# A fused attention and expert kernel whose main loop is emitted in the order of planned times

## The chip, the cores and the metric

The kernel runs on one core of one Trainium2 chip. The metric is the device time of one execution in microseconds (us), the median of three runs. In what follows PE is TensorE (matmuls), PEld its weight loads, DVE is VectorE, ACT is ScalarE, POOL is GpSimd and SP is SyncE, which issues DMAs. Each engine works its own instructions strictly in the order in which the program emitted them; engines wait for each other by semaphores.

## What is computed

```python
qn = q / (norm(q, axis=1) + 1e-6);  kn = k / (norm(k, axis=1) + 1e-6)
a = softmax(kn.transpose(0, 2, 1) @ qn / tau)          # per batch, 256 x 256
x = (v @ a).reshape(12032, 256)                        # 2 batches of 6016 tokens
h = x @ w_in                                           # 256 -> 2048
g = maximum(h, 0) + alpha * minimum(h, 0)
out = g @ w_out                                        # 2048 -> 256
```

All tensors are fp32.

## The kernel before, in words

The kernel folds the 256 x 256 attention matrix of a batch into `w_in`, so that only two large products per token are left. Each fp32 operand is split into a high part (a rounding cast) and a low part (the difference), and every product is three matmul passes (`passes`, lines L115, L116, L117; the plain second product has them at L830).

**Tiles and items.** The 12032 tokens are 24 tiles of 500 or 504 tokens (12 a batch), and the 2048 hidden features are 8 pairs of 128-blocks. One tile with one pair is an *item*; there are 192, numbered i = 8 t + j for tile t and pair j. The first product of an item is a scheme of seven half-width products instead of eight. The second product is plain (twelve 500-column matmuls) in tiles 0 to 12 and 23, and in tiles 13 to 22 (`S_TILES`) it is seven products in the items with even j (*S items*) and plain in those with odd j.

**The steps of item i**, by function:

- PE `pe_a` (six 250-column matmuls into PSUM tile q), ACT `copies` (q to the accumulators r0, L605, and to p7, L606), PE `pe_b` (six into r0), DVE `add_p7(i, 0)` (r0 + p7 into r1, L622).
- one loop step later: PE `pe_c` (six, into r1 and r0; it needs `add_p7(i, 0)`), DVE `add_p7(i, 1)` (L622, needs pe_c), PE `pe_d` (three, into r0; it may start only when `add_p7(i, 1)` has read r0), then for each half `act_n` (ACT, L635) and `dve_g` (DVE, L644), which make g.
- two loop steps later: the split of g. Plain: `g_high` (ACT, gh, L653) and `g_low` (DVE, gl, L657). S items: `x_high`, `x_low` (xh, xl), `g_sums` (three DVE sums into t), `t_low` (ACT, and a DMA issued by POOL), `t_high` (ACT, L722, tgh).
- three and four loop steps later (`LAG = 3`): the second product, in two halves: `stage2`'s five and seven matmuls for a plain tile, `s2_first` and `s2_second` in the tiles 13 to 22, which sum into the PSUM banks X0 to X3.

**Tile ends.** A tile of S_TILES ends with `combine` (ACT copy of X2, L786; DVE L787, L788, L793, which give c) and `finish_out` for two halves (DVE L800, into ob, then the store); only then are the banks free for the next tile. These stand in the items j = 2 and j = 3 of the next tile. Beside them the v data of a later tile are prepared: `v_sums` (DVE), `v_high` (ACT L343, and two DMAs issued by POOL), `v_low` (DVE L349).

**What sets the order.** Nothing reorders the program (`manual_schedule`). The loop over items emits the calls in a fixed sequence written by hand; work beside the main line (weights, norms of batch 1, v) is put on lists `side`, `early` and `late` by item number. So each engine's queue is the projection of this text on that engine.

Of the kernel before, what the change touches and what calls it, by code (L numbers as in the profile page):

```python
# [25 lines left out]
def fused_kernel(
# [637 lines left out]
    ws, xs_t, ts_t, tt_t, started, cb_t = [], {}, {}, {}, set(), {}  # L664
# [23 lines left out]
    def g_sums(i):

        g = g_t[i]  # L690
        h = half_of(i)
# [151 lines left out]
    with tc.manual_schedule():  # L843
# [133 lines left out]

        at_item(NPAIR, a1.evac)
        i = NPAIR + 4
        for p in range(len(pieces)):  # L980
# [16 lines left out]
        at_item(i, lambda: (a1.sums_T(), a1.norms()))  # L997
        at_item(i + 2, bcast1)
        at_item(i + 3, lambda: a1.exps())
        at_item(i + 5, transposes1)  # L1000
        assert i + 5 <= last0 - 3, (i, last0)
        for j in range(NPAIR):

            i = last0 + 2 + 11 * j // 7
# [6 lines left out]
            at_item(i + 1, lambda j=j: m_split(a1, j))
        for n in range(len(S_J)):
            at_item(last0 + (14, 16, 19, 21)[n], s_weights, n)
        early, late = {}, {}
        for t in S_TILES:
            i = (t + 1) * NPAIR - 1 + LAG
            late[i] = [lambda t=t: combine(t)]
            early[i + 1] = [lambda t=t: finish_out(t, 0)]
# [18 lines left out]
        def pe_s2(s2):  # L1037
            if s2 is not None:
                next(s2, None)
            else:  # L1040
                pe_fill()

        for i in range(NI + LAG):

# [4 lines left out]
            if s_two:
                x_high(i - 2)  # L1050
                g_sums(i - 2)
            elif two:
                g_high(i - 2, 1)
                g_high(i - 2, 0)
                g_low(i - 2, 1)
            if new:
                pe_a(i)
                copies(i)
            if one:
                pe_c(i - 1)  # L1060
                add_p7(i - 1, 1)
            if s_two:
                x_low(i - 2)
            elif two:
                g_low(i - 2, 0)
            if in_s(i - LAG - 1):
                s2_second(i - LAG - 1)
            if s2 or i < LAG:
                pe_s2(s2)
            if one:  # L1070
                act_n(i - 1, 1)
                dve_g(i - 1, 1)
            for f in early.get(i, []):
                f()
            if s_two:
                t_low(i - 2)
            if one:
                pe_d(i - 1)
            if new:
                pe_b(i)  # L1080
                add_p7(i, 0)
            if one:
                act_n(i - 1, 0)
                dve_g(i - 1, 0)
            if s_two:
                t_high(i - 2)
            for f, args in side.get(i, []):
                f(*args)
# [41 lines left out]
```

## Time and profile before

| | us |
|---|---|
| median of 3 timed runs | 1160.81 (1156.49 to 1161.18) |
| the profiled execution's own time | 1163.18 |
| its span in the profile | 1161.4 |
| PE busy in it | 1122.4 |
| DVE busy | 921.3 |
| ACT busy | 843.5 |

The profile is of one execution. Of the table, the span is the stretch from the first to the last instruction; the execution's own time is 1.8 us longer. The busy time of PE is the union of its matmuls with ends that are modelled, since they overlap in the array.

### The profile page before, as it was taken

How to read it: one execution, taken by the hardware profiler on the slowest of the kernel's cores; microseconds unless marked ns; L12 is line 12 of the kernel's file. 1: busy time of each engine (PE TensorE's matmuls, PEld its weight loads, DVE VectorE, ACT ScalarE, POOL GpSimd, SP SyncE). 2: the span in 40 equal slices, each digit the busy share in tenths (PEclk: the TensorE clock that was granted, in tenths of full speed). 3: DMA queues.
4: the chain of work that ended last, by engine and by line, in shares of the span. 5: the costliest groups of instructions: out<-in, count | busy, mean ns of one | idle time of the engine just before them, and what ended most of it. 6: DMA issues, size and time to landing. Idle time of an engine off the chain costs nothing.

```text
span 1161.4 us, 19221 instructions
## 1 busy us (share of the span) xinstructions
PE 1122.4 (97%) x7284; PEld 1022.3 (88%) x7284; DVE 921.3 (79%) x1693; ACT 843.5 (73%) x1498; POOL 92.8 (8%) x118
## 2 busy tenths in 40 slices
PE   9999999999999999999999989999999999999988
PEld 8888888988988988899898878988988989889887
DVE  6798876777777777777798888888988888988865
ACT  6788677777777767667777677767767677777664
POOL 0000000000000000000002241011011011011000
PEclk9999999999999999999999999999999999999999
DMA  9996122232232011101101033343343343333310
GB/s 333 361 337 220 36 72 89 72 106 74 79 99 79 27 36 54 27 28 54 36 19 37 19 89 81 77 94 71 79 101 71 73 91 78 82 87 76 70 36 19
DMA packets 54589, 103.59 MB, mean 89 GB/s; under 512 B 5088, under 2 KB 30944, under 8 KB 54496
## 3 DMA queue, kind: packets, MB, share of 16 engines
q1 hardware_dynamic: 36224, 70.01, 17.8%
q0 software_dynamic: 18272, 32.34, 13.9%
q8 instruction: 58, 0.95, 0.4%
q14 instruction: 35, 0.29, 0.1%
HBM read 57.68 MB, written 12.32 MB: 60 GB/s over the span
## 4 chain that ended last, share of the span: by engine, by line
PE 79%; DVE 11%; ACT 7%; issue 2%; DMA 0%; SPq 0%; ACTq 0%; DVEq 0%
PE o L830 23%; PE r L115 8%; PE r L117 8%; PE r L116 8%; PE S L401 6%; PE X L115 5%; PE X L117 4%; PE X L116 4%; PE q L116 3%; PE q L115 3%; PE q L117 3%; ACT g L635 2%; DVE r L622 2%; DVE gl L657 2%; DVE g L644 1%
## 5 line engine op out<-in xcount | busy, mean ns | idle before, releaser
L635 ACT ACTIVATE g<-r,salpha 128x500 f32<-128x500 f32 (+1 forms) x384 | 260.6, 680 | 137.4 <-DVE r L622 82.1
L644 DVE SCALAR_TENSOR_TENSOR g<-r,sgn,g 128x500 f32<-128x500 f32 (+1 forms) x384 | 282.8, 736 | 36.8 <-ACT g L635 36.7
L830 PE MATMUL o<-gh,wo 128*128 128x500 f32 (+2 forms) x904 | 296.5, 389 | 3.0 <-DVE ob L800 3.0
L115 PE MATMUL r<-vs,m 128*128 128x250 f32 (+1 forms) x960 | 272.9, 284 | 22.8 <-DVE r L622 22.7
L117 PE MATMUL r<-vs,m 128*128 128x250 f32 (+1 forms) x960 | 268.6, 280 | 0.0
L116 PE MATMUL r<-vs,m 128*128 128x250 f32 (+1 forms) x960 | 268.5, 280 | 0.0
L622 DVE TENSOR_TENSOR r<-r,p 128x250 f32<-128x250 f32 (+1 forms) x384 | 163.2, 425 | 128.5 <-PE r L117 125.0
L657 DVE TENSOR_TENSOR gl<-g,gh 128x500 fp32r<-128x500 f32 (+1 forms) x304 | 206.1, 678 | 27.9 <-ACT gh L653 26.5
L115 PEld LDWEIGHTS r<-vs,m 128*128 128x128 f32 x960 | 182.0, 190 | 41.5 <-DVE r L622 34.7
L653 ACT CAST gh<-g 128x500 fp32r<-128x500 f32 (+1 forms) x304 | 177.0, 612 | 32.1 <-DVE g L644 31.0
L116 PEld LDWEIGHTS r<-vs,m 128*128 128x128 f32 x960 | 182.0, 190 | 4.7
L830 PEld LDWEIGHTS o<-gh,wo 128*128 128x128 f32 x904 | 162.0, 188 | 26.6 <-DVE ob L800 3.8
L117 PEld LDWEIGHTS r<-vs,m 128*128 128x128 f32 x960 | 181.9, 189 | 0.0
L830 PE MATMUL o<-gl,wo 128*128 128x500 f32 (+2 forms) x452 | 175.4, 388 | 0.0
L605 ACT COPY r<-q 128x500 f32<-128x500 f32 (+1 forms) x192 | 109.4, 570 | 60.4 <-PE q L117 60.3
L115 PE MATMUL q<-vs,m 128*128 128x250 f32 (+1 forms) x384 | 110.1, 287 | 0.0
L116 PE MATMUL q<-vs,m 128*128 128x250 f32 (+1 forms) x384 | 109.1, 284 | 0.6 <-DVE vs L349 0.6
L117 PE MATMUL q<-vs,m 128*128 128x250 f32 (+1 forms) x384 | 108.9, 284 | 0.3 <-DVE m L111 0.3
L830 PEld LDWEIGHTS o<-gl,wo 128*128 128x128 f32 x452 | 84.9, 188 | 13.6
L341 POOL DMA_DIRECT2D vs<-vt x46 | 33.6, 733 | 669.7 <-PE q L117 393.2
L116 PEld LDWEIGHTS q<-vs,m 128*128 128x128 f32 x384 | 74.7, 194 | 6.9 <-DVE vs L349 0.9
L115 PEld LDWEIGHTS q<-vs,m 128*128 128x128 f32 x384 | 74.3, 194 | 6.1
(144 smaller groups left out, 1772.3 us busy)
## 6 DMA issues: line engine op xcount, KB each, us to landing
tgl<-t POOLq DMA_DIRECT2D x28, 500.0 KB, 4.6
kqT<-kqT_dram SPq DMA_DIRECT2D x20, 512.0 KB, 3.6
kq<-k_dram SPq DMA_DIRECT2D x39, 256.0 KB, 5.6
kq<-q_dram SPq DMA_DIRECT2D x39, 256.0 KB, 5.7
v<-vT_dram SPq DMA_DIRECT2D x16, 500.0 KB, 4.3
vs<-vt POOLq DMA_DIRECT2D x32, 250.0 KB, 2.6
outT_dram<-ob SPq DMA_DIRECT2D x30, 250.0 KB, 2.0
tgl<-t POOLq DMA_DIRECT2D x12, 504.0 KB, 4.6
```

Source lines behind the costliest of these rows:

```text
L115: nc.tensor.matmul(out, wh, xh, start=first, stop=False, **s)
L116: nc.tensor.matmul(out, wh, xl, start=False, stop=False, **s)
L117: nc.tensor.matmul(out, wl, xh, start=False, stop=last, **s)
L341: nc.gpsimd.dma_start(out=v_spl[t][:, 0, sl, :h], in_=x)
L401: nc.tensor.matmul(self.S[cc], t[:, 0, j, cc * P : cc * P + P], t[:, 1, j, :], start=ci == 0 and j == 0 and not (self.shared and cc), stop ...
L605: nc.scalar.copy(r_t[i][0][:, :, :h], x[:, 0:1, :h].broadcast_to([P, 2, h]))
L622: nc.vector.tensor_tensor(out=r[1][:, n, :h], in0=r[0][:, 1, :h], in1=p7_t[i][:, :h], op=ALU.add)
L635: nc.scalar.activation(blocks(g_t[i], i, 2 * fi, 2 * fi + 2), r_t[i][fi][:, :, : half_of(i)], AF.Copy, scale=salpha[:, f : f + 1],)
L644: nc.vector.scalar_tensor_tensor(out=g, in0=r_t[i][fi][:, :, : half_of(i)], scalar=sgn[:, f : f + 1], in1=g, op0=ALU.mult, op1=ALU.max,)
L653: nc.scalar.copy(gs_t[i][0][:, fi, :w], g_t[i][:, fi * w : fi * w + w])
L657: nc.vector.tensor_tensor(out=gs_t[i][1][:, fi, :w], in0=g_t[i][:, fi * w : fi * w + w], in1=f32(gs_t[i][0][:, fi, :w]), op=ALU.subtract,)
L830: nc.tensor.matmul(o, x, y, start=first, stop=last or shared, skip_group_check=shared)
```

## The change

The loop no longer calls the steps; it puts each into a list `plan` with a planned time (item number times `PERIOD`, plus an offset), and at the end the list is sorted by that time and called. The offsets come from a table `ORDER` with one entry for each kind of loop step: *plain* (tiles 0 to 12 and 23), *sums* (the step in which the S item i - 2 is split) and *none* (the other steps of tiles 13 to 22). The numbers serve as sort keys only: no instruction is added, removed or moved to another engine. `g_sums` is cut into its three instructions, `combine` and `s_weights` into two calls each, so that the parts can be placed apart. In the loop steps of the plain kind, pe_c stands ahead of pe_a; before, pe_a was ahead of pe_c in every step.

```diff
+PERIOD = 5.0
+SIDE = 3.7
+ORDER = {
+    "plain": dict(
+        pe_c=0.0, add=(3.0, 0.1), high=(0.3, 0.2), pe_a=0.7, copy=0.8, low=(1.1, 1.0),
...
+TILE = dict(copy=3.42, sums=4.41, out0=1.24, out1=3.0)
...
-    def combine(t):
-
+    def combine_copy(t):
         h = tiles[t][2] // 2
         c = cb_t[t] = raw.tile([P, 2 * TW], F32, tag="raw", name=f"c{t}")
+        nc.scalar.copy(c[:, 3 * h : 4 * h], bank(t, 2)[:, :h])
+
+    def combine(t):
+
+        h = tiles[t][2] // 2
+        c = cb_t[t]
         p2, p3 = bank(t, 2), bank(t, 3)
         tt = nc.vector.tensor_tensor
-        nc.scalar.copy(c[:, 3 * h : 4 * h], p2[:, :h])
...
+        plan = []
+
+        def put(i, at, f, *args):
+            plan.append((i * PERIOD + at, len(plan), f, args))
+
+        def side(i, f, *args):
+            put(i, SIDE, f, *args)
...
         for n in range(len(S_J)):
-            at_item(last0 + (14, 16, 19, 21)[n], s_weights, n)
-        early, late = {}, {}
+            i = last0 + (14, 16, 18, 20)[n]
+            put(i, SIDE, s_weights, n)
+            put(i + 2, SIDE, s_weights_split, n)
         for t in S_TILES:
             i = (t + 1) * NPAIR - 1 + LAG
-            late[i] = [lambda t=t: combine(t)]
-            early[i + 1] = [lambda t=t: finish_out(t, 0)]
-            late[i + 1] = [lambda t=t: finish_out(t, 1)]
+            put(i, TILE["copy"], combine_copy, t)
+            put(i, TILE["sums"], combine, t)
+            put(i + 1, TILE["out0"], finish_out, t, 0)
+            put(i + 1, TILE["out1"], finish_out, t, 1)
...
-            when = (0, 1, 1, 1, 2, 4, 5, 6) if t > 1 else (4, 4, 4, 5, 5, 6, 7, 7)
...
+            if t == 1:
+                when = [(i, SIDE) for i in (4, 4, 4, 5, 5, 6, 7, 7)]
+            elif t - 1 < S_TILES[0]:
+                when = [(i, SIDE) for i in (1, 1, 2, 2, 2, 4, 5, 6)]
+            else:
+                when = V_STEPS
...
+            o = ORDER["plain" if not in_s(i) and not in_s(i - 1) else "sums" if s_two else "none"]
...
+            if new:
+                put(i, o["pe_a"], pe_a, i)
+                put(i, o["copy"], copies, i)
+                put(i, o["pe_b"], pe_b, i)
+                put(i, o["add"][0], add_p7, i, 0)
+            if one:
+                put(i, o["pe_c"], pe_c, i - 1)
+                put(i, o["add"][1], add_p7, i - 1, 1)
+                put(i, o["pe_d"], pe_d, i - 1)
...
+        for _, _, f, args in sorted(plan, key=lambda x: x[:2]):
+            f(*args)
```

Three places show what the sort makes of it. In each row the numbers behind a tile's name are its item (or tile) and a buffer number.

**PE, a plain loop step (item 18, tile 2).** Before:

```order
L115 MATMUL q18_1844<-vs2_1324,m0_2_631 128x252
...
L115 MATMUL r1_17_1796<-vs2_1324,m0_1_601 128x252
...
L115 MATMUL r0_17_1795<-vs2_1324,m0_1_601 128x252
...
L830 MATMUL o0_1_1474<-gh15_1783,wo_112 128x504
L830 MATMUL o0_1_1474<-gl15_1784,wo_112 128x504
L830 MATMUL o0_1_1474<-gh15_1783,wo_112 128x504 x2
L830 MATMUL o0_1_1474<-gl15_1784,wo_112 128x504
L115 MATMUL r0_17_1795<-vs2_1324,m0_1_601 128x252
...
L115 MATMUL r0_18_1851<-vs2_1324,m0_2_631 128x252
```

And with the change:

```order
L143 MATMUL r1_17_1798<-vs2_1376,m0_1_601 128x252
...
L143 MATMUL r0_17_1797<-vs2_1376,m0_1_601 128x252
...
L143 MATMUL q18_1848<-vs2_1376,m0_2_631 128x252
...
L867 MATMUL o0_1_1474<-gh15_1786,wo_112 128x504
L867 MATMUL o0_1_1474<-gl15_1787,wo_112 128x504
L867 MATMUL o0_1_1474<-gh15_1786,wo_112 128x504 x2
L867 MATMUL o0_1_1474<-gl15_1787,wo_112 128x504
L143 MATMUL r0_17_1797<-vs2_1376,m0_1_601 128x252
...
L143 MATMUL r0_18_1855<-vs2_1376,m0_2_631 128x252
```

pe_c (r1_17, r0_17) has moved ahead of pe_a (q18), so between pe_c and pe_d (the r0_17 row behind the o0 rows) there are now pe_a's six matmuls and the five of the second product, and between pe_a and pe_b (r0_18) pe_c's six are gone.

**DVE, the end of tile 15 (items 130 and 131).** Before:

```order
L644 SCALAR_TENSOR_TENSOR g129_8560<-r0_129_8474,sgn_108,g129_8560 128x500
L787 TENSOR_TENSOR c15_8588<-X2_15_8139,c15_8588 128x252
L788 TENSOR_TENSOR c15_8588<-X3_15_8172,c15_8588 128x504
L793 TENSOR_TENSOR c15_8588<-X3_15_8172,c15_8588 128x252
L657 TENSOR_TENSOR gl129_8594<-g129_8560,gh129_8593 128x500
L622 TENSOR_TENSOR r1_130_8536<-r0_130_8535,p7_130_8537 128x250
L657 TENSOR_TENSOR gl129_8594<-g129_8560,gh129_8593 128x500
L644 SCALAR_TENSOR_TENSOR g130_8624<-r1_130_8536,sgn_108,g130_8624 128x500
L800 TENSOR_TENSOR ob15_8627<-X0_15_8132,c15_8588 128x504
L622 TENSOR_TENSOR r1_131_8606<-r0_131_8605,p7_131_8607 128x250
```

And with the change:

```order
L672 SCALAR_TENSOR_TENSOR g129_8558<-r0_129_8472,sgn_108,g129_8558 128x500
L824 TENSOR_TENSOR c15_8577<-X2_15_8139,c15_8577 128x252
L825 TENSOR_TENSOR c15_8577<-X3_15_8170,c15_8577 128x504
L830 TENSOR_TENSOR c15_8577<-X3_15_8170,c15_8577 128x252
L650 TENSOR_TENSOR r1_130_8542<-r0_130_8541,p7_130_8543 128x250
L837 TENSOR_TENSOR ob15_8615<-X0_15_8132,c15_8577 128x504
L685 TENSOR_TENSOR gl129_8585<-g129_8558,gh129_8584 128x500
L672 SCALAR_TENSOR_TENSOR g130_8613<-r1_130_8542,sgn_108,g130_8613 128x500
L685 TENSOR_TENSOR gl129_8585<-g129_8558,gh129_8584 128x500
L837 TENSOR_TENSOR ob15_8615<-X1_15_8180,c15_8577 128x504
L650 TENSOR_TENSOR r1_131_8602<-r0_131_8601,p7_131_8603 128x250
```

The add for item 130 (r1_130) comes straight behind the three sums instead of behind a gl, and both outputs (ob15) stand ahead of the add for item 131.

**ACT, the same place.** Before:

```order
L635 ACTIVATE g129_8560<-r0_129_8474,salpha_109 128x500
L722 CAST tgh128_8563<-t128_8524 128x1000
L343 CAST vs17_8453<-v17_8208 128x250
L343 CAST vs17_8453<-v17_8208 128x2x250
L786 COPY c15_8588<-X2_15_8139 128x252
L653 CAST gh129_8593<-g129_8560 128x500 x2
L605 COPY r0_131_8605<-q131_8598 128x2x250
```

And with the change:

```order
L663 ACTIVATE g129_8558<-r0_129_8472,salpha_109 128x500
L816 COPY c15_8577<-X2_15_8139 128x252
L681 CAST gh129_8584<-g129_8558 128x500 x2
L633 COPY r0_131_8601<-q131_8593 128x2x250
L634 COPY p7_131_8603<-q131_8593 128x250
L663 ACTIVATE g130_8613<-r1_130_8542,salpha_109 128x500
L371 CAST vs17_8452<-v17_8216 128x250
L371 CAST vs17_8452<-v17_8216 128x2x250
L755 CAST tgh128_8568<-t128_8520 128x1000
L663 ACTIVATE g130_8613<-r0_130_8541,salpha_109 128x500
```

The copy of X2 now stands directly behind the activation, and the v casts and tgh one loop step later, ahead of the second activation of item 130.

## Rows read from the trace of the kernel before

**Rows 1.** First part of the page: busy time, share of span, instructions.

```profile
PE 1122.4 (97%) x7284; PEld 1022.3 (88%) x7284; DVE 921.3 (79%) x1693; ACT 843.5 (73%) x1498; POOL 92.8 (8%) x118
```

**Rows 2.** Four windows: length; busy PE, PEld, DVE, ACT, POOL; PEclk; DMA.

```profile
658.10:702.40 44.30, 40.46 (x281) 36.95 (x280) 37.29 (x62) 33.00 (x57) 15.91 (x18) 1.00 0.31 71
702.40:1102.60 400.20, 380.74 (x2703) 357.13 (x2702) 339.41 (x622) 291.84 (x495) 44.79 (x54) 0.97 0.37 81
859.00:860.20 1.20, 1.20 (x7) 1.20 (x7) 1.13 (x3) 0.21 (x1) 0.00 (x0) 0.50 0.32 118
1117.90:1128.00 10.10, 7.09 (x40) 5.75 (x39) 6.37 (x12) 3.85 (x7) 0.00 (x0) 1.00 0.13 50
```

**Rows 3.** Waits of PE and its loads, 92:656 us: total, times, longest.

```profile
PE r L115 <- DVE r L622: 6.7, 12, 1.4
...
PEld r L115 <- DVE r L622: 13.8, 18, 1.8
```

**Rows 4.** Timeline, item 19 of the plain tiles: start, duration, instruction, [idle before].

```profile
194.98 0.28 PE L115 MATMUL q<-vs,m 128*128 128x252 f32 x1
...
198.04 0.39 PE L115 MATMUL r<-vs,m 128*128 128x252 f32 x1 [0.34 <-DVE r L622]
...
197.56 0.42 DVE L622 TENSOR_TENSOR r<-r,p 128x252 f32<-128x252 f32 x1
...
196.31 1.14 ACT L653 CAST gh<-g 128x504 fp32r<-128x504 f32 x2
197.34 0.59 ACT L605 COPY r<-q 128x504 f32<-128x504 f32 x1
```

**Rows 5.** Part 5 of the page: the copy out of q, all 192.

```profile
L605 ACT COPY r<-q 128x500 f32<-128x500 f32 (+1 forms) x192 | 109.4, 570 | 60.4 <-PE q L117 60.3
```

**Rows 6.** Timeline of TensorE, starts of items 142 and 144.

```profile
870.24 0.28 PE L115 MATMUL q<-vs,m 128*128 128x250 f32 x1
870.36 0.28 PE L116 MATMUL q<-vs,m 128*128 128x250 f32 x1
...
880.34 0.28 PE L115 MATMUL q<-vs,m 128*128 128x250 f32 x1
```

**Rows 7.** Timeline of ACT, DVE, PE, end of tile 15 (items 130, 131).

```profile
807.35 1.03 ACT L722 CAST tgh<-t 128x1000 fp32r<-128x1000 f32 x1
808.27 0.92 ACT L343 CAST vs<-v 128x250 fp32r<-128x250 f32 x2
809.08 0.38 ACT L786 COPY c<-X 128x252 f32<-128x252 f32 x1
...
807.49 0.74 DVE L644 SCALAR_TENSOR_TENSOR g<-r,sgn,g 128x500 f32<-128x500 f32 x1 [0.22 <-ACT g L635]
809.48 0.42 DVE L787 TENSOR_TENSOR c<-X,c 128x252 f32<-128x252 f32 x1 [1.26 <-ACT c L786]
809.94 0.68 DVE L788 TENSOR_TENSOR c<-X,c 128x504 f32<-128x504 f32 x1
810.66 0.42 DVE L793 TENSOR_TENSOR c<-X,c 128x252 f32<-128x252 f32 x1
811.00 0.67 DVE L657 TENSOR_TENSOR gl<-g,gh 128x500 fp32r<-128x500 f32 x1
811.58 0.42 DVE L622 TENSOR_TENSOR r<-r,p 128x250 f32<-128x250 f32 x1
...
812.06 0.38 PE L115 MATMUL r<-vs,m 128*128 128x250 f32 x1 [1.33 <-DVE r L622]
...
814.19 0.38 PE L115 MATMUL X<-xh,wo 128*128 128x250 f32 x1 [0.81 <-DVE ob L800]
```

**Rows 8.** Timeline of TensorE in item 187, first of two stops.

```profile
1122.33 0.49 PE L830 MATMUL o<-gh,wo 128*128 128x500 f32 x1 [1.50 <-DVE ob L800]
1122.66 0.39 PE L830 MATMUL o<-gl,wo 128*128 128x500 f32 x1
1122.89 0.39 PE L830 MATMUL o<-gh,wo 128*128 128x500 f32 x1
```

More of the change, by code (lines that the diff above doesn't have):

```diff
@@ L22 @@
 FILL = 7
+PERIOD = 5.0
[3 more added lines that the diff above has]
+        pe_c=0.0, add=(3.0, 0.1), high=(0.3, 0.2), pe_a=0.7, copy=0.8, low=(1.1, 1.0),
+        s2=(1.4, 3.8), act_n=(3.1, 1.5), dve_g=(3.2, 1.6), pe_d=2.5, pe_b=2.9,
+    ),
+    "none": dict(
+        high=(0.34, -0.31), low=(1.77, 2.51), pe_a=0.3, copy=0.4, pe_c=0.7, add=(3.68, 0.8),
+        s2=(1.39, 4.11), act_n=(4.2, 0.93), dve_g=(4.3, 2.0), pe_d=2.8, pe_b=3.04,
+    ),
+    "sums": dict(
+        x_high=0.84, g_sums=(0.02, 0.2, 2.04), pe_a=0.35, copy=1.53, pe_c=0.7, add=(3.9, 0.93),
+        x_low=2.34, s2=(1.53, 4.71), act_n=(3.17, 1.7), dve_g=(4.3, 2.85), t_low=2.66, pe_d=3.1,
+        pe_b=2.29, t_high=7.52,
+    ),
+}
+TILE = dict(copy=3.42, sums=4.41, out0=1.24, out1=3.0)
+V_STEPS = (
+    (0, 4.5),
+    (1, 4.5),
+    (1, 4.5),
+    (1, 5.18),
+    (2, 6.44),
+    (4, 5.19),
+    (5, 4.55),
+    (6, 2.57),
+)
 @with_exitstack
@@ L663, in fused_kernel @@
     S_J = (0, 2, 4, 6)
[L664 removed]
+    sw_t, ws, xs_t, ts_t, tt_t, started, cb_t = {}, [], {}, {}, {}, set(), {}
     def in_s(i):
@@ L996, in fused_kernel @@
         i = (i + 2 * len(pieces) + NPAIR - 1) // NPAIR * NPAIR + 4
[L997 to L1000, printed above, removed]
+        side(i, lambda: (a1.sums_T(), a1.norms()))
+        side(i + 2, bcast1)
+        side(i + 3, a1.exps)
+        side(i + 5, transposes1)
         assert i + 5 <= last0 - 3, (i, last0)
@@ L1035, in pe_fill, with pe_s2 @@
                 a1.chunk_pe(ci)
[L1037 to L1040, printed above, removed]
+        s2_t = {}
+        def pe_s2(i):
+            if i < 0:
                 pe_fill()
+                return
+            if i not in s2_t:
+                s2_t[i] = stage2(i)
+            next(s2_t[i], None)
         for i in range(NI + LAG):
             new, one, two = i < NI, 0 <= i - 1 < NI, 0 <= i - 2 < NI
-            s2 = stage2(i - LAG) if i >= LAG and not in_s(i - LAG) else None
@@ L1052, in fused_kernel @@
             elif two:
-                g_high(i - 2, 1)
-                g_high(i - 2, 0)
-                g_low(i - 2, 1)
+                for fi in range(2):
+                    put(i, o["high"][fi], g_high, i - 2, fi)
+                    put(i, o["low"][fi], g_low, i - 2, fi)
             if new:
-                pe_a(i)
-                copies(i)
+                put(i, o["pe_a"], pe_a, i)
+                put(i, o["copy"], copies, i)
+                put(i, o["pe_b"], pe_b, i)
+                put(i, o["add"][0], add_p7, i, 0)
@@ L1059, in fused_kernel @@
             if one:
[L1060 to L1065, printed above, removed]
-            if in_s(i - LAG - 1):
[L1067 to L1088, printed above, removed]
+                put(i, o["pe_c"], pe_c, i - 1)
+                put(i, o["add"][1], add_p7, i - 1, 1)
+                put(i, o["pe_d"], pe_d, i - 1)
+                for fi in range(2):
+                    put(i, o["act_n"][fi], act_n, i - 1, fi)
+                    put(i, o["dve_g"][fi], dve_g, i - 1, fi)
@@ L1089, in fused_kernel @@
+            if in_s(i - LAG - 1):
+                put(i, o["s2"][0], s2_second, i - LAG - 1)
             if in_s(i - LAG):
-                s2_first(i - LAG)
+                put(i, o["s2"][1], s2_first, i - LAG)
             else:
-                pe_s2(s2)
-            for f in late.get(i, []):
-                f()
+                for at in o["s2"] if not in_s(i - LAG - 1) else (o["s2"][1],) * 2:
+                    put(i, at, pe_s2, i - LAG)
             if i == LAG:
-                pe_fill()
+                put(i, PERIOD, pe_fill)
```

63 lines of the change are left out of this document (34 added, 29 removed).

## The prediction

> **What bounds the kernel now.** I read the first part of the page, then where PE stops, then what stood in the releasing engine's queue. PE is busy 1122.4 of 1161.4 us, DVE 921.3, ACT 843.5 [rows 1], so TensorE sets the time, and only two things can be gained: its stops, and matmuls at the lower clock. The 39.0 us in which PE is not busy understate this: in item 131 the row shows 1.33 us idle [rows 7], but that counts from the modelled end of the matmul before, which lasts 0.39 while the next could start 0.23 behind it [rows 8]; so the stop costs 1.49.
>
> Here the Trainium skill (Perfetto Trace Analysis, Identifying the Most-Contended Engine) has a rule: matmul busy time is a bad measure of the room left, since matmuls overlap; weight-load busy time is better. By matmul busy no more than 39.0 us could come back; by weight loads, busy 88%, there is more. The trace sides with the page, as the sum below shows.
>
> Where are the stops? In three places.
>
> Tiles 13 to 22: from tile 14 to tile 22 (702.4 to 1102.6) nine tiles take 400.2 us [rows 2]. Two undisturbed items take 880.34 - 870.24 = 10.10 us [rows 6], nine tiles of four such pairs 363.6. So 36.6 us, 4.1 a tile, are lost, all around items j = 3 and j = 4, where the previous tile ends. Rows 7 show one such end. DVE finishes g at 808.23, then sits idle 1.26 us for ACT's copy of X2, because ACT has tgh (1.03) and the v casts (0.92) ahead of it. The sums (0.42, 0.68, 0.42) and a gl follow, so `add_p7(130, 1)` starts at 811.58, while PE's pe_d has been due since about 810.57 and starts at 812.06. Then the next tile's first product into X0 waits for the output (0.81 idle at 814.19). After two such stops the granted clock is 0.50 for about a microsecond at some tile ends (859.0 to 860.2 [rows 2]), that is 1.2 instead of 2.4 GHz; the mean over the nine tiles is 0.97.
>
> Last tile: item 187 takes 10.1 us [rows 2]. Its 21 matmuls of 250 columns at 0.116 us [rows 6] and 18 of 500 at 0.23 [rows 8] make 6.6, so 3.5 are lost, waiting for the outputs of tile 22 [rows 8].
>
> Plain tiles: between 92 and 656 us PE waits for an add (L622) 6.7 us by its own rows and 13.8 by its weight loads' [rows 3]; between the two I take 11 for all, refill included. Rows 4 show the pattern in item 19, which repeats in five other tiles at j = 3: ACT is late (T squares, v casts, ob copies, then gh), DVE's gl waits for gh, and `add_p7(18, 1)` is queued behind that gl though it could have gone earlier; pe_d follows the add at 198.04, 0.5 late.
>
> **The change part by part.** No instruction is added or removed, so PE's own work stays; every term is a stop.
>
> *Tile ends, items 130 and 131 with the new queues.* ACT: the copy (0.38), where tgh began at 807.35, ends about 807.75, before DVE is ready. On DVE the sums start at about 808.15 and each next one 0.46 and 0.72 later, as in rows 7; instructions that don't need each other overlap by 0.08 (from 810.66 a sum of 0.42 and a gl of 0.67 take 0.92). So the third sum takes 0.34, and `add_p7(130, 1)` runs from 809.66 to 810.09, before pe_d is due at 810.57: the first stop is gone. Then out0 (as wide as a gl: 0.59 to the next start; ready 810.67, and X0's first product is due at 811.6: second stop gone), gl, g 0.66, gl, out1, so `add_p7(131, 0)` runs from 813.02 to 813.44, while its reader pe_c(131) is due at 813.35: a stop of 0.15 with the semaphore. That is the new lateness: the outputs now stand ahead of that add. With full durations in place of the overlapped starts the stop is 0.75; with a few tenths less it is nought. I take 0.3 a tile, 2.7 for nine, and no clock drop: 36.6 - 2.7 = 33.9 gained, bounds 36.6 and 18 (half comes back).
>
> The v casts and tgh that left this place go to the next loop step on ACT: 1.95 us ahead of an activation whose g is needed by the copy of item 132 only about 2 us later. The cover is ACT's slack: 291.84 busy of 400.2 [rows 2]. If it is gone, pe_b of item 132 waits some tenths; in the 0.3.
>
> *Last tile.* In item 187 the second product of tile 23 is now emitted behind both outputs and at the end of PE's step. DVE: sums, add, two gl, out0 (1.52, 0.34, 1.18, 0.67) end about 3.9 us after the step's start, out1, behind another dve_g, about 5.3; PE needs them at 3.8 (its 27 other matmuls) and 5.2. Left 0.2: gain 3.3, bounds 0 and 3.5.
>
> *Tile 13 (658.1 to 702.4).* 44.3 us [rows 2] against four pairs less 1.1 (item 107 has only nine second-product matmuls) = 39.3: 5.0 lost. There is little PE work to hide behind, ACT has ob copies, v casts and ws in two items, and POOL sums run beside DVE. I work out a stop of 1.3 us in item 107 and one of about 1.2 in 108 (r0's copy behind xh). Gain 2.5, bounds 0 and 5.0. The second part of the weights' sums moves up to two items later; its reader is three loop steps behind it.
>
> *Plain steps.* pe_c ahead of pe_a gives `add_p7(i - 1, 1)` 0.70 us more (six matmuls at 0.116) before pe_d, and the add now stands ahead of both gl. So it no longer waits for gh, and the 11 us go, with 0.6 of a wait for v in item 8. In their place r0's copy can be late: pe_b starts 1.5 us after pe_a instead of 2.2. In item 19 the copy ends 197.93 [rows 4], pushed perhaps 0.14 later, and pe_b is due at 197.87 (194.98 and 0.70, 0.70, 1.15, 0.35 of matmuls): 0.25 lost with refill instead of 0.6. Six such items 1.6, items 3, 69 and 91 with 0.6 to 0.8 each, two small ones: 4.1 left. Gain 7.5, bounds 0 and 11.6.
>
> *In steps without side work* nothing should appear. ACT stands ready for q: the copies waited 60.3 us in all for it and take 0.57 [rows 5], so r0 is ready about 0.8 us after pe_a, due at 1.5. In the steps called sums, pe_b stands ahead of pe_d, three matmuls (0.35 us) earlier, behind 2.1 us of other matmuls. No row shows the wait; bounds 0 and 40 times 0.35 = 14. I take 0, nearest to rows 5.
>
> *Queues.* The v DMAs on POOL go up to a loop step later; their reader is three loop steps on, some 15 us. Stores on SP only follow the outputs.
>
> Sum: 33.9 + 3.3 + 2.5 + 7.5 = 47.2. The profiled execution's own 1163.2 becomes 1116.0. It lies 2.4 above the runs' median, so a timed median may be a little lower: I say 1115.
>
> **The rivals.**
>
> *DVE becomes the bound in tiles 14 to 22* (0.20). It is busy 339.4 us there [rows 2]; in 363.6 that is 93% in one in-order queue, and each wait for ACT then pushes the next add. For it: the margins at a tile end are tenths. Against: the busy time falls on j = 1 to 3 and there is slack in the other items. If half of each tile end's loss returns, 18 - 2.7 = 15 us more: 1130.
>
> *PSUM is the limit, not the order* (0.06). The stop at X0 [rows 7] and those of item 187 [rows 8] wait for a bank of the previous tile, and recur at each tile end; if the bank cannot come free earlier, 9 times 0.97 (0.81 idle and 0.16 as above) and 0.7 of clock, and 3.3, stay: 1115 + 18 = 1133. The Trainium skill (Perfetto Trace Analysis, Optimization Strategy) says of consistent bubbles that they can mean too little PSUM for the next tile. Against it in the rows: what delays the output is DVE's late queue, not the bank's last matmul.
>
> *The stops only move* (0.03), because DVE or ACT has no earlier time to give: 1160. Against: DVE sat idle 1.26 us in the very place.
>
> *Slower: pe_c at the head of a plain step* (0.04). It needs `add_p7(i, 0)` of the step just ended, and only 1.6 us of matmuls (seven at 0.23) lie between instead of 2.3. The add is queued on DVE behind a dve_g that waits for ACT, which waits for q, now 0.70 later. I find it ready 0.7 us ahead: behind pe_a come 0.17 until its result, three ACT instructions of about 0.6 [rows 4], a dve_g of 0.74 and the add, 0.42 [rows 7], 3.1 in all, and pe_c is due 3.8 behind it (1.15, 0.35, 0.70 and 1.61 of matmuls). If it were late in the 104 plain steps by more than 47.2 / 104 = 0.45 us, the change loses; at 0.55 late the time is 1116 + 57 = 1173.
>
> **How the numbers follow.** The forecast has 0.67, and its own range is 1106 (all stops gone) to 1125. The range for 8 in 10 reaches to both middle rivals, 1105 to 1137. About 0.5% (6 us) is what a measurement can tell from no change: faster 0.93, same 0.03, slower 0.04.
>
> **What would show it.** After: nine tiles from 14 on in 364 to 370 us, PEclk 1.00 there; no PE r waiting for L650 (the add) at pe_d in plain tiles, small waits for r0's copy (L633) at j = 3 instead; item 187 under 7 us; tile 13 still with stops. Wrong it would be with a wait of PE at every pair or every plain step, for the add ahead of pe_c, or for r0 in the sums steps; or with DVE above 95% and stops of a microsecond or more left at tile ends.

## The result and the profile after

The changed kernel takes 1113.76 us (median of 4 runs, 1113.69 to 1113.88) against 1158.65 for the kernel before on the same chip (1154.92 to 1161.18): a ratio of 0.9615, 95% interval 0.9583 to 0.9647. The forecast was 1115, and faster. The profiled execution has a span of 1112.1 us, 49.3 under that of before. The medians differ by less, 44.9, since the kernel before varies with the clock: eleven of its executions on one chip take 1155.6 to 1163.7 us, the shortest at a mean granted clock of 0.995 and the longest at 0.988.

First the engines and the chain that ended last, from the page; to compare with [rows 1]:

```profile
PE 1104.1 (99%) x7284; PEld 1014.2 (91%) x7284; DVE 906.7 (82%) x1693; ACT 840.4 (76%) x1498; POOL 91.8 (8%) x118
...
PE 96%; DVE 2%; ACT 1%; DMA 0%; issue 0%; SPq 0%; ACTq 0%; DVEq 0%
```

The chain is TensorE alone but for 4%, so little is left that another engine could give back. The span has fallen by 49.3 although PE's busy time fell by only 18.3. Two things that went were counted as busy: the matmuls at the lower clock, 10.9 us in the nine tiles 14 to 22 by the spacing of their starts, and at each stop what the modelled end of the matmul before hides. The lower clock shows in this window at the end of tile 16, before the change (length; busy PE, PEld, DVE, ACT, POOL; PEclk; DMA):

```profile
857.90:861.30 3.40, 3.40 (x18) 3.40 (x17) 2.48 (x5) 1.43 (x3) 0.00 (x0) 0.50 0.41 151
```

It lasts about 3 us, at seven of the nine tile ends; the prediction had read off about a microsecond.

The Trainium skill (Perfetto Trace Analysis, Identifying the Most-Contended Engine) says that matmul busy time does not tell how close a kernel is to its limit, because pipelined matmuls look smaller in the trace. In the outcome the trace agrees: PE was not busy for 39.0 us and 49.3 came back. But the larger part of what busy time hid here is the clock, not the overlap.

Then four windows (length; busy PE, PEld, DVE, ACT, POOL; PEclk; DMA): items 0 to 103, tile 13, tiles 14 to 22, item 187; to compare with [rows 2]:

```profile
92.30:649.80 557.50, 555.95 (x3542) 502.68 (x3541) 430.76 (x813) 411.12 (x782) 23.36 (x31) 1.00 0.21 63
649.80:692.40 42.60, 40.52 (x281) 36.97 (x280) 36.79 (x62) 32.70 (x58) 21.12 (x24) 1.00 0.33 74
692.40:1056.90 364.50, 364.50 (x2702) 346.66 (x2701) 329.58 (x622) 294.21 (x495) 44.75 (x54) 1.00 0.40 88
1073.00:1079.60 6.60, 6.60 (x42) 5.89 (x41) 4.92 (x10) 3.32 (x6) 0.00 (x0) 1.00 0.23 81
```

The nine tiles take 364.5 instead of 400.2, item 187 takes 6.6 instead of 10.1, tile 13 takes 42.6 instead of 44.3, and items 0 to 103 take 557.5 instead of 566.1 (the first q matmul of item 0 stood at 92.0 before, that of item 104 at 658.1). These gains, 35.7, 3.5, 1.7 and 8.6, make 49.5; the start-up lost 0.3. Of the 35.7, by the spacing of the starts, about 24.6 are stops and 10.9 the clock. The matmul that follows the first one behind a stop starts about 0.10 late as well; this is the *refill* of the texts below.

The end of tile 15, now in items 130 and 131 (timeline: start, duration, instruction, [idle before]; ACT, DVE, PE apart); to compare with [rows 7]:

```profile
788.34 0.36 ACT L816 COPY c<-X 128x252 f32<-128x252 f32 x1
...
788.48 0.74 DVE L672 SCALAR_TENSOR_TENSOR g<-r,sgn,g 128x500 f32<-128x500 f32 x1
789.13 0.41 DVE L824 TENSOR_TENSOR c<-X,c 128x252 f32<-128x252 f32 x1
...
790.63 0.42 DVE L650 TENSOR_TENSOR r<-r,p 128x250 f32<-128x250 f32 x1
790.95 0.67 DVE L837 TENSOR_TENSOR ob<-X,c 128x504 f32<-128x504 f32 x1
...
793.96 0.41 DVE L650 TENSOR_TENSOR r<-r,p 128x250 f32<-128x250 f32 x1
...
788.89 0.28 PE L143 MATMUL q<-vs,m 128*128 128x250 f32 x1
...
791.66 0.28 PE L143 MATMUL r<-vs,m 128*128 128x250 f32 x1
...
792.71 0.28 PE L143 MATMUL X<-xh,wo 128*128 128x250 f32 x1
...
794.46 0.35 PE L143 MATMUL r<-vs,m 128*128 128x250 f32 x1
```

The copy of X2 is over when VectorE ends g, so the first sum follows without an idle gap, and the add for pe_d starts 2.15 behind the start of that g (forecast 2.17) and ends 0.6 before pe_d. Neither pe_d nor the first product into X0 has an idle time in its row. What is left is pe_c(131) at 794.46: its add ends at 794.37, and with the semaphore pe_c comes 0.07 late. That is the lateness that the prediction named (worked out 0.15, taken 0.3); it is 0.07 to 0.15 with little refill at eight other ends.

### The profile page after: what moved, and what is told of

The parts are those of the page before. It is cut to its first block, busy times and chain, and to the rows that moved or that the text cites. A ratio compares the mean times of both kernels' runs of the same rounds, so it can differ in the third digit from the quotient of the medians.

```text
span 1112.1 us, 19275 instructions
## 1 busy us (share of the span) xinstructions
PE 1104.1 (99%) x7284; PEld 1014.2 (91%) x7284; DVE 906.7 (82%) x1693; ACT 840.4 (76%) x1498; POOL 91.8 (8%) x118
## 4 chain that ended last, share of the span: by engine, by line
PE 96%; DVE 2%; ACT 1%; DMA 0%; issue 0%; SPq 0%; ACTq 0%; DVEq 0%
PE o L867 27%; PE r L143 10%; PE r L145 10%; PE r L144 10%; PE S L429 7%; PE X L143 6%; PE X L145 6%; PE X L144 6%; PE q L144 4%; PE q L143 4%; PE q L145 4%; PE pm L569 1%; DMA kqs<-q_dram 0%; DVE g L672 0%; DVE vs L377 0%
## 5 line engine op out<-in xcount | busy, mean ns | idle before, releaser
L681 ACT CAST gh<-g 128x500 fp32r<-128x500 f32 (+1 forms) x304 | 181.1, 612 | 42.1 <-DVE g L672 40.2
L685 DVE TENSOR_TENSOR gl<-g,gh 128x500 fp32r<-128x500 f32 (+1 forms) x304 | 197.2, 679 | 4.7 <-ACT gh L681 4.6
L144 PE MATMUL q<-vs,m 128*128 128x250 f32 (+1 forms) x384 | 107.4, 280 | 0.0
L143 PE MATMUL q<-vs,m 128*128 128x250 f32 (+1 forms) x384 | 107.3, 280 | 0.0
L145 PE MATMUL q<-vs,m 128*128 128x250 f32 (+1 forms) x384 | 107.1, 279 | 0.0
L429 PE MATMUL S<-kq 128*128 128x256 f32 x332 | 74.7, 379 | 0.0
L144 PEld LDWEIGHTS q<-vs,m 128*128 128x128 f32 x384 | 72.4, 189 | 1.8
```

What stands on the lines that cost most here:

```text
L143: nc.tensor.matmul(out, wh, xh, start=first, stop=False, **s)
L144: nc.tensor.matmul(out, wh, xl, start=False, stop=False, **s)
L145: nc.tensor.matmul(out, wl, xh, start=False, stop=last, **s)
L429: nc.tensor.matmul(self.S[cc], t[:, 0, j, cc * P : cc * P + P], t[:, 1, j, :], start=ci == 0 and j == 0 and not (self.shared and cc), stop ...
L681: nc.scalar.copy(gs_t[i][0][:, fi, :w], g_t[i][:, fi * w : fi * w + w])
L685: nc.vector.tensor_tensor(out=gs_t[i][1][:, fi, :w], in0=g_t[i][:, fi * w : fi * w + w], in1=f32(gs_t[i][0][:, fi, :w]), op=ALU.subtract,)
```

## The experiments

All times are medians. The changed kernel was timed on one chip (a spread of 0.2 us) and the experiments on others, where the kernel before had medians of 1160.8 to 1162.1. Where an experiment leaves a stage as it is, the stage takes the same time to 0.1 us (the nine tiles 364.5 to 364.6 in `e2_s_only`, `e3_pe_c_first`, `e4_add_first` and `i2_dup_late`), but the start-up varies by 1.6, so differences of a microsecond or two are read from stages.

**Halves.** `e1_plain_only` keeps the new plain table, and gives the two other tables, the tile ends, the v casts and the weight sums of tile 13 their former order; `e2_s_only` is the reverse.

```diff
 # e2: the plain table in the former order (numbers are sort keys)
-        pe_c=0.0, add=(3.0, 0.1), high=(0.3, 0.2), pe_a=0.7, copy=0.8, low=(1.1, 1.0),
-        s2=(1.4, 3.8), act_n=(3.1, 1.5), dve_g=(3.2, 1.6), pe_d=2.5, pe_b=2.9,
+        high=(0.02, 0.01), low=(0.3, 0.03), pe_a=0.1, copy=0.11, pe_c=0.2, add=(0.91, 0.21),
+        s2=(0.4, 3.8), act_n=(1.0, 0.5), dve_g=(1.01, 0.51), pe_d=0.8, pe_b=0.9,
...
-                when = [(i, SIDE) for i in (1, 1, 2, 2, 2, 4, 5, 6)]
+                when = [(i, SIDE) for i in (0, 1, 1, 1, 2, 4, 5, 6)]
```

> The plain table alone (and the last tile's place with it); the two tables of tiles 13 to 22, the tile ends and the v casts stand as before. My account, in which each place pays for itself: the plain steps give back 7.5 and the last tile up to 3.3, so 8 to 11 us under the kernel before, about 1148, and tiles 14 to 22 stay at 400 us with a granted clock of 0.97. Rival, that all comes from one common cause (the loop as a whole): a much larger share of the 45 us, under 1135.

> The other half: the tables of tiles 13 to 22, the tile ends and the v casts as in the change, the plain steps as before. My account: 7 to 8 us over the changed kernel, about 1121, with tiles 14 to 22 at 364 to 365 us and the waits of TensorE for the add in items j = 3 of the plain tiles back. Rival, that the plain order also carries into the later tiles: more than 15 us over it.

Measured 1150.65 (1149.64 to 1151.80; ratio 0.9916, 0.9890 to 0.9942) and 1122.58 (1122.29 to 1124.65; ratio 0.9680, 0.9649 to 0.9711). The halves give 10.1 and 38.2 against 1160.8, in sum 48.3 where the whole gives 47.0: in the main each place pays for itself. Two windows of e1 (tiles 14 to 22, item 187) and two of e2 (items 0 to 103, item 187) show where it is less simple:

```profile
695.70:1092.60 396.90, 377.51 (x2702) 353.92 (x2701) 339.29 (x622) 291.77 (x495) 44.73 (x54) 0.98 0.37 81
1108.70:1116.10 7.40, 6.82 (x42) 5.76 (x41) 5.01 (x10) 3.32 (x6) 0.00 (x0) 1.00 0.19 69
```

```profile
91.40:656.10 564.70, 558.06 (x3541) 501.30 (x3540) 432.63 (x813) 416.43 (x782) 23.59 (x31) 1.00 0.21 62
1078.40:1087.00 8.60, 6.86 (x41) 5.93 (x40) 6.60 (x13) 3.92 (x7) 0.00 (x0) 1.00 0.18 62
```

In e1 the nine tiles take 3.3 less than before, though their stops sum to 25.5 by the starts in both: the lower clock came at five ends instead of seven. So nothing shows that the plain table earned this part. That e2's 8.8 over the changed kernel is near the 8.6 of the plain items is in part chance: only 7.2 of it lies there (the other 1.4 is a stop at item 103 that went in e2 too, with GpSimd's weight work put off), and 2.0 in item 187, which needs both halves: 10.1 before, 7.4 in e1, 8.6 in e2, 6.6 in the changed kernel.

**Which edit earned the plain steps' 8.6.** `e3_pe_c_first` puts only the add behind the first gl again, `e4_add_first` only pe_a ahead of pe_c.

```diff
 # e3
-        ... high=(0.3, 0.2), ... low=(1.1, 1.0),
+        ... high=(0.3, 0.02), ... low=(1.1, 0.05),
 # e4
-        pe_c=0.0, ... pe_a=0.7,
+        pe_c=0.0, ... pe_a=-0.1,
```

> The change, but in plain steps the add for pe_d stands behind the first gl again, as before; pe_c stays ahead of pe_a. If the add's place on VectorE is what earned the plain steps' gain: pe_d is due no later than before, gl still waits for gh, so the stops of 0.5 at j = 3 are back, and the r0 copy's stops may stay beside them: 4 to 11 us over the changed kernel. If pe_c's place earned it: within 1 us of the changed kernel.

> The change, but in plain steps pe_a stands ahead of pe_c again, as before; the add stays ahead of both gl. If the add's place earned the gain: the add ends about 0.6 behind pe_c's last matmul and pe_d is due 1.15 behind it, so no stop at pe_d, and the r0 copy has 0.7 more before pe_b, so its stops of 0.2 go too: 0 to 2 us under the changed kernel. If pe_c's place earned it: 4 to 8 us over it.

Measured 1121.14 (1120.92 to 1121.49), 7.4 over the changed kernel, and 1115.42 (1115.21 to 1115.68), 1.7 over it. So the add's place is the edit that counts; but e4 came out above, not below. Its rows, of PE at the starts of items 8 and 103 and of item 19, say why:

```profile
136.92 0.39 PE L144 MATMUL q<-vs,m 128*128 128x252 f32 x1 [0.62 <-DVE vs L377]
...
646.33 0.38 PE L145 MATMUL q<-vs,m 128*128 128x252 f32 x1 [0.48 <-DVE m L139]
...
196.62 0.59 ACT L633 COPY r<-q 128x504 f32<-128x504 f32 x1
...
197.25 0.39 PE L143 MATMUL r<-vs,m 128*128 128x252 f32 x1
```

With pe_a first, q waits for the v and the M that are just being made: 0.78 instead of 0.08 at item 8, and 0.65 with a refill of 0.10 at item 103. That is what pe_c ahead of pe_a is worth, 1.4 in two places. And in item 19 r0's copy still ends just behind the time at which pe_b is due: the same stop of 0.09 and 0.10 as in the changed kernel, though pe_a stands 0.7 earlier.

**Which edit earned the tile ends' 35.7.** `e5_act_old` undoes ScalarE's part, `e6_dve_old` a part of VectorE's order, `e8_both_old` both; the order on TensorE stays new.

```diff
 # e5
-        pe_b=2.29, t_high=7.52,
+        pe_b=2.29, t_high=4.35,
-TILE = dict(copy=3.42, sums=4.41, out0=1.24, out1=3.0)
+TILE = dict(copy=4.4, sums=4.41, out0=1.24, out1=3.0)
-    (2, 6.44),
+    (2, 4.36),
 # e6, in "none"
-        ... low=(1.77, 2.51), ... add=(3.68, 0.8), ... act_n=(4.2, 0.93),
+        ... low=(1.77, 2.51), ... add=(3.68, 1.9), ... act_n=(4.2, 1.95),
```

> The change, but at tile ends ScalarE's queue stands as before: tgh and the two v casts ahead of the copy of X2, which is again behind the other work of its step; VectorE's order stays new. My account, that the late copy is what starts the chain of stops: VectorE idles again about 1.3 us for it, its slack before pe_d is 0.6 to 0.7, so pe_d is 0.7 to 1.3 late and the first product into X0 a little too, in nine or ten tile ends, with the clock's drop behind it: 8 to 20 us over the changed kernel, about 1127. Rival, that VectorE's order alone earned it: within 2 us of the changed kernel.

> The change, but in the steps of tiles 13 to 22 called none the add for pe_d stands behind out0 and a gl on VectorE, as a gl stood before; ScalarE's queue stays new. My account: at a tile end the add ends at about 2.0 us after the sums instead of 0.4, pe_d about 0.65 late with refill 0.8, at nine or ten places, and no stop in the other steps: 4 to 10 us over the changed kernel. Rival, that the copy on ScalarE alone earned it: within 2 us.

> Both halves of the tile end undone at once: ScalarE's queue as in the one experiment and VectorE's add as in the other; the order on TensorE and the rest of the tables stay new. One alone cost 12.1 and 8.0 us in tiles 14 to 22. If the two are one chain (the late copy makes VectorE idle, and everything queued ahead of the add comes on top), the costs add up, or more with the clock's drop: 20 to 36 us over the changed kernel, 1134 to 1150, and with it most of the 36 lost before. If they are two covers of the same stop: 12 to 15 us over it, about 1127, and the rest of the 36 is owed to TensorE's own order.

Measured 1126.94 (1126.53 to 1128.04), 1124.18 (1123.51 to 1125.31) and 1155.29 (1153.94 to 1156.21): 13.2, 10.4 and 41.5 over the changed kernel. The nine tiles take 376.6, 372.5 and 400.4 us; below each of the first two stands its pe_d at the end of tile 15, and for e5 its next pe_c:

```profile
693.00:1069.60 376.60, 368.44 (x2702) 346.01 (x2701) 330.79 (x624) 290.91 (x495) 44.75 (x54) 1.00 0.39 86
...
795.89 0.38 PE L143 MATMUL r<-vs,m 128*128 128x250 f32 x1 [0.62 <-DVE r L650]
...
799.22 0.38 PE L143 MATMUL r<-vs,m 128*128 128x250 f32 x1 [0.27 <-DVE r L650]
```

```profile
694.10:1066.60 372.50, 368.36 (x2703) 345.35 (x2702) 329.14 (x622) 294.03 (x495) 44.76 (x54) 1.00 0.40 87
...
795.84 0.38 PE L143 MATMUL r<-vs,m 128*128 128x250 f32 x1 [0.45 <-DVE r L650]
```

```profile
697.70:1098.10 400.40, 380.36 (x2702) 356.53 (x2702) 331.25 (x622) 294.49 (x495) 44.78 (x54) 0.97 0.37 81
...
808.00:811.20 3.20, 3.20 (x16) 3.20 (x17) 2.67 (x5) 1.18 (x2) 0.00 (x0) 0.50 0.13 45
```

In e5 my number held, but not all of its parts: the first product into X0 is not late and the clock does not drop; instead pe_c at j = 4 is 0.43 late. In e6, tile 13 adds 2.2, which takes the time just over the range.

The two edits together bring back 35.9, as much as was gained, with TensorE's new order in place. They do not bring back the former queue: before, a tile end had a stop of 1.5 at pe_d and one of 1.0 at X0; in e8, where out0 stands ahead of the late add, it has one of 2.4 at pe_d and none at X0. So e8 shows that a late copy and a late add suffice for a loss of this size; that it comes out so near the former one is in part chance. One alone costs 12.1 or 8.0, both together not 20.1 but 35.9: of the 15.8 on top, 12.1 are matmuls at the lower clock, by the spacing of their starts, and under 4 are stops. The timeline of `e8_both_old` at the end of tile 15 (DVE, PE) shows how the stop adds up:

```profile
802.63 0.74 DVE L672 SCALAR_TENSOR_TENSOR g<-r,sgn,g 128x500 f32<-128x500 f32 x1
804.62 0.42 DVE L824 TENSOR_TENSOR c<-X,c 128x252 f32<-128x252 f32 x1 [1.25 <-ACT c L816]
...
806.13 0.67 DVE L837 TENSOR_TENSOR ob<-X,c 128x504 f32<-128x504 f32 x1
806.72 0.67 DVE L685 TENSOR_TENSOR gl<-g,gh 128x500 fp32r<-128x500 f32 x1
807.31 0.42 DVE L650 TENSOR_TENSOR r<-r,p 128x250 f32<-128x250 f32 x1
...
802.62 0.28 PE L143 MATMUL q<-vs,m 128*128 128x250 f32 x1
...
807.78 0.54 PE L143 MATMUL r<-vs,m 128*128 128x250 f32 x1 [2.22 <-DVE r L650]
```

The late copy starts the sums 1.34 later (1.99 behind g's start instead of 0.65), the two instructions ahead of the add cost 1.19 more, and pe_d has 0.56 of spare time (0.61 in the changed kernel, less 0.05 between the add's end and pe_d), which counts once. Alone, 0.78 and 0.62 are left (by the starts, with the 0.16 that the modelled end hides, 0.78 and 0.61 at this tile end). Together it would be 1.97, and the starts give 2.38; the rest is that VectorE's g comes 0.42 later against TensorE's q than in the changed kernel (802.63 and 802.62; there 788.48 and 788.89), for which I have no cause. Behind this stop 16 matmuls run at a granted clock of 0.50 (1.2 GHz), 0.21 instead of 0.12 apart; behind the stops of 0.6 to 0.9 of the other two the clock stays at 1.00. So my forecast of 20 to 36 for both held in these tiles; with tile 13, which takes 5.7 more (stops of 3.7 and 1.9), the time passed it.

**Is VectorE the bound in tiles 14 to 22?** `e7_dve_load` does the third g sum twice, with the same result.

```diff
+                put(i, o["g_sums"][2] + 0.01, g_sums, i - 2, 2)
```

> The change with one more sum on VectorE in each S item: the third of the g sums is done twice with the same result, 0.42 us, 36 times in tiles 14 to 22. VectorE goes from 329.6 to about 345 of 364.5, 95%. If VectorE's total were the bound there, each of these pairs would pay a good part of it, 10 to 15 us. My account, in which only the lateness at a tile end counts: pe_d's margin of 0.65 takes most of it, the add ahead of pe_c at j = 4, already 0.07 late, pays up to 0.4 a tile, so 2 to 5 us over the changed kernel and nothing at j = 5 to 7.

Measured 1117.49 (1117.15 to 1118.35), 3.7 over; the nine tiles take 367.5, 3.0 more:

```profile
693.80:1061.30 367.50, 366.39 (x2702) 346.73 (x2701) 340.77 (x659) 295.71 (x495) 44.75 (x54) 1.00 0.40 88
```

VectorE is busy 11.2 more and 93% of the stretch, and 3.0 is paid, at pe_c of the items j = 4 (0.26 to 0.31 and a refill of 0.10 each); of the other items two have a stop, 0.09 and 0.18. VectorE's total is not the bound; its lateness at one place is.

**The slower rival, brought on.** In plain steps `i2_dup_late` does one gl twice, with the same result, and puts the add that pe_c needs behind it and behind the second dve_g.

```diff
-        pe_c=0.0, add=(3.0, 0.1),
+        pe_c=0.0, add=(3.25, 0.1),
...
+                if not in_s(i) and not in_s(i - 1):
+                    put(i, 2.95, g_low, i - 2, 0)
```

> The mechanism of the slower rival, brought on: in plain steps one gl is done twice (0.65 us on VectorE, the same result) and the add that pe_c needs stands behind it and behind the second dve_g. From the rows of the changed kernel that add ends at 297.15 and pe_c starts at 298.12; with both it ends at about 298.4, so pe_c is 0.35 late and 0.45 with refill, in 104 plain steps: 36 to 60 us over the changed kernel, 1150 to 1174, at or above the kernel before. If the margin was larger than the rows show, or VectorE catches up, under 15 us over it.

Measured 1155.90 (1154.60 to 1156.47), 42.1 over. A plain item takes 5.53 instead of 5.18; DVE and PE in one of them, and a window of 310 us of such items:

```profile
304.27 0.67 DVE L685 TENSOR_TENSOR gl<-g,gh 128x500 fp32r<-128x500 f32 x1
304.86 0.73 DVE L672 SCALAR_TENSOR_TENSOR g<-r,sgn,g 128x500 f32<-128x500 f32 x1
305.51 0.42 DVE L650 TENSOR_TENSOR r<-r,p 128x250 f32<-128x250 f32 x1
...
305.98 0.38 PE L143 MATMUL r<-vs,m 128*128 128x250 f32 x1
```

```profile
140.00:450.00 310.00, 303.61 (x1835) 257.35 (x1834) 242.21 (x448) 216.42 (x411) 9.97 (x14) 1.00 0.23 69
```

The add ends 0.05 before pe_c starts, and pe_c is 0.2 late with 0.10 of refill in most steps, more at j = 3. VectorE is busy for 78% of the stretch: its total does not set the time, but what stands ahead of this one add (a doubled gl and a dve_g) loses 42.

**Tile 13.** The changed kernel's largest stop left is in item 109 (DVE, POOL, PE):

```profile
676.29 3.21 DVE L377 TENSOR_TENSOR vs<-v,vs 128x252 fp32r<-128x252 f32 x2
679.43 0.41 DVE L650 TENSOR_TENSOR r<-r,p 128x252 f32<-128x252 f32 x1
...
676.19 1.34 POOL L718 TENSOR_TENSOR ws<-sw,ws 128x512 fp32r<-128x512 f32 x1
677.45 1.51 POOL L708 TENSOR_TENSOR sw<-wo 128x512 f32<-128x512 f32 x1
...
679.90 0.38 PE L143 MATMUL r<-vs,m 128*128 128x252 f32 x1 [1.14 <-DVE r L650]
```

Two v_low take 3.21 while GpSimd works on the second product's weights. `h0_pool_early` moves that work ahead of tile 13.

```diff
-            i = last0 + (14, 16, 18, 20)[n]
+            i = last0 + (13, 14, 15, 16)[n]
...
-            put(i + 2, SIDE, s_weights_split, n)
+            put(i + 1, SIDE, s_weights_split, n)
```

> The change with the second product's weight sums on GpSimd one to four items earlier (items 101 to 104, their split one item behind), so that they lie ahead of tile 13. If these sums are what makes two v_low on VectorE take 3.21 us in item 109 (elsewhere 1.00) and r0's copy wait behind ws on ScalarE: the stops of 1.3 and 0.6 in items 109 and 108 go, 1 to 2.5 us under the changed kernel, 1111.3 to 1112.8. If the same sums slow gl and the splits of M in tile 12 instead: no gain, or up to 2 us over it.

Measured 1116.88 (1115.49 to 1118.06): 3.1 over (2.3 of it in tile 13), worse than either account. The timeline, of ACT, DVE and PE in item 105, and of the same two v_low:

```profile
655.83 0.62 ACT L717 CAST ws<-sw 128x512 fp32r<-128x512 f32 x1 [3.10 <-POOL sw L712]
656.35 0.68 ACT L663 ACTIVATE g<-r,salpha 128x504 f32<-128x504 f32 x1
...
659.93 0.58 PE L143 MATMUL r<-vs,m 128*128 128x252 f32 x1 [2.84 <-DVE r L650]
...
679.64 1.00 DVE L377 TENSOR_TENSOR vs<-v,vs 128x252 fp32r<-128x252 f32 x2
```

The first account was right on its point: beside an idle GpSimd the pair takes 1.00, its stop is gone, and r0's copy is late by 0.20 instead of 0.58. But the split, now one item behind instead of two, makes ScalarE stand still 3.10 for GpSimd's last sum, with an activation queued behind it, and TensorE stops for 3.0, with the lower clock behind it.

**Three small stops taken up.** `h1_three` moves the norms of batch 1 three items later, the second output of a tile behind the add that pe_c needs, and the v casts of plain tiles one item later.

```diff
-TILE = dict(copy=3.42, sums=4.41, out0=1.24, out1=3.0)
+TILE = dict(copy=3.42, sums=4.41, out0=1.24, out1=3.7)
...
+        i += 3
         side(i, lambda: (a1.sums_T(), a1.norms()))
...
-                when = [(i, SIDE) for i in (1, 1, 2, 2, 2, 4, 5, 6)]
+                when = [(i, SIDE) for i in (1, 1, 2, 2, 3, 4, 5, 6)]
```

> The change with three small stops taken up. The norms of batch 1 three items later, where no v work stands on VectorE: 1.0 less at item 69. The second output of a tile behind the add that pe_c waits for: nine stops of 0.07 to 0.15 with refill go, 0.9 to 1.4 less, since the bank's next product is due some 2 us later. The v casts of the plain tiles one item later, away from the T squares and the output copies: six stops of 0.1 to 0.2 less, 1.0. Together 2 to 3.4 us under the changed kernel, 1110.4 to 1111.8. Rival, that each only moves its stop to another place: within 0.7 us of it.

Measured 1112.77 (1112.50 to 1113.24), 1.0 under, half of the least that I expected. The v casts did it in the plain tiles (no stop is left at j = 3) and the outputs in the nine tile ends (363.9 instead of 364.5). But the norms made new stops of 1.2 in place of 1.0, and in item 187 the last tile's second output, at the new place, came 0.84 late. `h2_final` mends both.

```diff
-        side(i, lambda: (a1.sums_T(), a1.norms()))
+        side(i - 5, lambda: (a1.sums_T(), a1.norms()))
...
-            put(i + 1, TILE["out1"], finish_out, t, 1)
+            put(i + 1, TILE["out1"] + 0.7 * (t < S_TILES[-1]), finish_out, t, 1)
...
-                when = [(i, SIDE) for i in (1, 1, 2, 2, 2, 4, 5, 6)]
+                when = [(i, SIDE) for i in (1, 1, 2, 2, 3, 4, 5, 6)]
```

> The version with three small stops taken up, mended where its trace showed a new one: the norms of batch 1 go five items earlier (a step j = 7 without v work) instead of three later, since there they and the exponentials made 1.2 of stops in place of 1.0; and the second output of the last S tile stays at its former place, since there it cost 0.84. My account: plain steps 1.6 to 2.3 under the changed kernel, nine tile ends 0.6, the last tile as in the change: 1110.8 to 1111.7. Rival, that the norms again move their stop to another place: 1111.8 to 1112.5.

Measured 1111.06 (1110.88 to 1111.75), a ratio to the kernel before of 0.9572 (0.9548 to 0.9597): 2.7 under the changed kernel and the fastest of all. In item 19 r0's copy now runs at 195.06 instead of 195.92, since the v casts no longer stand ahead of the two gh, and pe_b no longer waits for it.

## Why the prediction was right, point by point

*What bounds the kernel.* Right: every gain is a stop of TensorE that went, or its matmuls at the lower clock. How long the lower clock lasts was read too short (one microsecond for about three), which the sum did not need, since it took the whole loss by subtraction.

*Tile ends, 33.9 forecast, 35.7 measured.* Right in place and mechanism. The two edits named (the copy ahead of tgh and the v casts; the add ahead of gl and out0) are shown by `e8_both_old` to suffice for a loss of this size. Of the size, 10.9 of the 35.7 is the clock, which the account did not price apart, and the new stop at pe_c was taken as 0.3 a tile and is about 0.1, and with full clock.

*ScalarE's slack as the cover.* Right: with 294.2 of 364.5 us busy, no stop appeared where the v casts and tgh went.

*Last tile, 3.3 forecast, 3.5 measured.* Right; the 0.2 left did not come. By e1 and e2 it takes the plain table and the tile ends together.

*Tile 13, 2.5 forecast, 1.7 measured.* The term was too large. The two stops that I left in came at half their size: 0.68 instead of 1.3 in item 107, and 0.58 instead of 1.2 in item 108 (r0's copy). But the largest, 1.31 in item 109, was not in the sum: it is v_low beside GpSimd's sums. I had noted that POOL sums run beside DVE and worked out no price for it.

*Plain steps, 7.5 forecast, 8.6 measured.* The 4.1 left agree (by the starts of the matmuls, the stops over 0.06 sum to 4.1, without those of about 0.19 in items 0 to 4 that both kernels have); their parts less so, as the six at j = 3 are 0.9 instead of 1.6. The loss before was the mis-sized part: I took 11 between 6.7 and 13.8, and 8.6 and 4.1 make 12.7. The reason given for the r0 stops was wrong in one step: that pe_b starts 1.5 behind pe_a's end instead of 2.2. `e4_add_first` gives the 0.7 back and the stops stay; `h1_three` moves ScalarE's v casts and they go. Of the two edits, the add's place carries the term; the 0.70 that pe_c's place gives ahead of pe_d is worth little by itself, since in `e3_pe_c_first` the stop at item 19 is 0.5 as before, and its 1.4 comes from the waits for v and M. The wait for v in item 8 was right, 0.7 for 0.6, but a second one, for M in item 103, was missed.

*Nothing in steps without side work.* Right: undisturbed plain items take 5.18 as before, and no r0 stop shows in the sums steps of tiles 14 to 22.

*The rivals.* VectorE as the bound: refuted by `e7_dve_load`. The stops only move: refuted, since 49.3 came back. PSUM as the limit: refuted, since the first product into X0 has no idle time with the banks unchanged. The Trainium skill (Perfetto Trace Analysis, Optimization Strategy) says of consistent bubbles that they can mean too little PSUM; here they did not. Slower by pe_c at the head: real, with a margin of about 0.9 in the changed kernel (0.7 forecast); `i2_dup_late` passes it by 0.3 with the refill and loses 42, and is still 2 us under the shortest run of the kernel before beside it (1158.1).

## What to carry to other kernels

In strictly ordered queues ask of each instruction that another engine waits for what stands ahead of it, and how much spare time its reader has; put the ones with a waiting reader first, casts and outputs with two microseconds of slack behind. The spare time counts once, and a longer stop can bring the lower clock behind it: two edits that each seem to give little (8 and 12) held 36 between them here, 12 of it clock, so undo them together before dropping either. VectorE held TensorE up at 85% busy before, by its order, and at 93% with the order kept it cost 3.0.

## What the hardware showed that I had not expected

- VectorE beside GpSimd: the two v_low last 1.53 and 1.76 beside GpSimd's weight work in the changed kernel, by the row that gives the shortest, median and longest in ns, and 0.41 and 0.68 beside an idle GpSimd in `h0_pool_early`.

```profile
L377 DVE TENSOR_TENSOR vs<-v,vs x2: 1531/1646/1760, 676.3 to 677.7; 128x252 fp32r<-128x252 f32 x1, 128x504 fp32r<-128x504 f32 x1
```

  The times fit a wait better than a slower rate. GpSimd's two operations end at 677.53 and 678.96; a v_low that did all its work behind them would end at 677.94 and 679.64, and they end at 677.82 and 679.50. The Trainium skill (SBUF — State Buffer, Who interferes with whom) says that a VectorE instruction with both inputs in SBUF contends with a GpSimd instruction that reads SBUF, and that whichever issues second waits until the first ends. The trace agrees, to 0.14. The trace of the kernel before has the same waits (the same two v_low 1.55 and 0.94, and in item 103 a v_low and a gl of 1.77 each that take 0.67 elsewhere), and by the same sum each ends within 0.14; so the price that the prediction lacked for tile 13 could have been read there.
- The granted clock: at ends with stops of 2.4 us it was 0.50 over the next few us in eight of nine tiles of `e8_both_old`, and 1.00 behind a stop of 1.9 in its tile 13; in the kernel before, with stops of 1.5 and 1.0 at each end, it was 0.50 behind seven of nine. The ninth stop of `e8_both_old` was as long as the others (2.39) and cost no clock; what sets it apart is open.
